# Decode attention over two caches: engine programs rolled into loops over the 16 groups, with TensorE's first matmuls at the end of its program

## The chip, the cores and the metric

The kernel runs on one core of a Trainium2 chip. The metric is the device time of one execution in microseconds; every time below is in microseconds unless it says ns. A core has five engines that run their own instruction streams and meet on semaphores: TensorE (PE, matmuls into PSUM), VectorE (DVE), ScalarE (ACT), GpSimd (POOL) and SyncE (SP), which here issues nearly all transfers. Sixteen DMA engines, fed by a queue in the order of issue, carry the data.

## The reference

Two halves, A and B, do the same on data of their own: one token attends over 8192 cached positions with 32 heads of 128, and the two results of 512 numbers are put side by side.

```python
def _A_ref(x, k_cache, v_cache, wq, wo):      # B the same, with its own five inputs
    q = (x @ wq).reshape(B, Sq, H, Dh).transpose(0, 2, 1, 3)      # 1 x 32 heads x 1 x 128
    scores = jnp.einsum("bhqd,bhkd->bhqk", q, k_cache) * (Dh ** -0.5)
    p = _softmax(scores, axis=-1)
    o = jnp.einsum("bhqk,bhkd->bhqd", p, v_cache)
    return o.transpose(0, 2, 1, 3).reshape(B, Sq, H * Dh) @ wo    # 4096 -> 512
```

All inputs are bf16. The caches are 67 MB each, four of them; the weights `wq` and `wo` are 4 MB each, four of them.

## The kernel before

**Tiles.** Four heads make a group, so there are 16 groups (`NM`), eight for A and eight for B. A group's K (or V) is one tile of 128 partitions, 32 for each head, with 256 positions of 128 numbers on each partition: one transfer of 8 MB. Two K tiles are in the buffer `kn`, one V tile in `vn`. Below, K3 is the K tile of group 3, wqA the projection weights of A.

**One group n.** VectorE multiplies the K tile by the broadcast query in place, in four chunks of 64 positions (`plan_mul`, L353). TensorE adds up each chunk's products over the head dimension, 16 matmuls with the identity that leave 8 partial sums for a position (`plan_red`, L362). VectorE adds these eight (`plan_sr`, L373). Then come the maximum over a head (`plan_max`, `plan_gmax`: VectorE, a TensorE transpose, VectorE) and its broadcast (`plan_exp`: a small matmul, ScalarE), the four exponentials on ScalarE (L410), their sum (`plan_sum`, L415), the product with V on TensorE (`plan_pv`, L433, 64 matmuls), a ScalarE copy out of PSUM (`plan_acc`, L451), four turning matmuls (`plan_turn`, L459) and the scaling on VectorE (`plan_o`, L465).

**The start.** wqA and x come first; x is spread over the partitions with matmuls; the queries of A are made with `plan_q` (L331), in two halves of 16 matmuls. Each matmul fills only the 32 columns of one head slice, so that the four slices stand side by side in the array. ScalarE copies a half to `qbc` in one cast (L339). The queries of B are made in the middle of group 0, after its third reduction.

**The end.** A's output and the first 16 heads of B are multiplied by `wo` while the last V is on its way, with the accumulating rows packed four to the array (`plan_wo`, L533); the remaining heads follow as rows of a second layout (`plan_wo_rows`, L572), and VectorE writes the last row for the store.

**What sets the order.** A plan (`_Plan`) records the operations with what they need, and `_Loop` folds the recorded rounds into loops. On SyncE the order is wqA, x, K0, wqB, K1, V0, K2, V1, K3, V2 and so on. K(n+1) waits for the last reduction of group n-1, which frees its buffer; V(n) waits for the product with V(n-1), which frees `vn`. TensorE's order in a round is: three reductions of group n, the sum and value product of group n-1, the fourth reduction of group n, the turning matmuls of n-1, the maximum. Around the loops of VectorE and ScalarE stands a loop of two passes, of which the first skips its body; TensorE has a similar one of two passes.

```python
            plan_red(n, 2)
            plan_sr(n, 1)
            plan_mul(n, 3)
            plan_sr(n, 2)
            if n == 0:
                for j in range(QA // 4):
                    plan_q(1, j)
            else:
                plan_sum(n - 1)
                for t0, t1 in zip(VLAST, VLAST[1:]):
                    plan_pv(n - 1, t0, t1)
                plan_acc(n - 1)
            plan_red(n, 3)
```

Of the kernel before, what the change touches and what calls it, by code (L numbers as in the profile page):

```python
# [11 lines left out]
P = 128  # L12


class _Ctr:


    def __init__(self, nc, stack, name):
        self.sem = stack.enter_context(nc.semaphore(name))
        self.n = 0  # L20
        self.name = name


class _Plan:


    def __init__(self):
        self.prog = {"SP": [], "PE": [], "ACT": [], "DVE": [], "POOL": []}
        self.waited = {}

    def wait(self, eng, mark):
        if mark is None:
            return
        ctr, val = mark
        if val <= 0 or self.waited.get((eng, ctr.name), 0) >= val:
            return
        self.waited[(eng, ctr.name)] = val
        self.prog[eng].append((None, ctr, val))

    def op(self, eng, fn, ctr=None, needs=(), inc=1):  # L40

        for m in needs:
            self.wait(eng, m)
        self.prog[eng].append((fn, ctr, inc))
        if ctr is None:
            return None
        ctr.n += inc
        return ctr, ctr.n


def _emit(e, items, slot=None):
    for fn, ctr, k in items:
        if fn is None:
            e.wait_ge(ctr.sem, k)
        elif isinstance(fn, tuple):
            which, fns = fn
            if slot is None:
                fns[which](e).then_inc(ctr.sem, k)
            else:
                with e.If_eq(slot, 0):  # L60
                    fns[0](e).then_inc(ctr.sem, k)
                with e.Else():
                    fns[1](e).then_inc(ctr.sem, k)
        elif ctr is None:
            fn(e)
        else:
            fn(e).then_inc(ctr.sem, k)


def _steps(items):  # L70


    out, waits = [], []
    for it in items:
        if it[0] is None:
            waits.append(it[1:])
        else:
            out.append((waits, it))
            waits = []
    assert not waits  # L80
    return out


class _Loop:


    def __init__(self, e, rounds):
        self.e = e
        rounds = [_steps(r) for r in rounds]
        assert len({len(r) for r in rounds}) == 1  # L90
        early, self.body, self.last = [], [], []
        for k in range(len(rounds[0])):
            at = [r[k] for r in rounds]
            assert all(it[1:] == at[0][1][1:] for _, it in at)
            first, second, third = at[0][0], at[1][0], at[2][0]
            waits = []
            for (ctr, v), (_, w) in zip(second, third):
                d = w - v
                assert v - d >= 1
                waits.append((ctr, v - d, d))  # L100
            for n, (ws, _) in enumerate(at[1:], 1):
                assert [(c, v) for c, v in ws] == [(c, v + n * d) for c, v, d in waits]
            for ctr, v in first:
                same = [x for c, x, _ in waits if c is ctr]
                if not same:
                    early.append((None, ctr, v))
                else:
                    assert v <= same[0]
            self.body.append((waits, at[0][1]))
            self.last.append([(c, v + len(rounds) * d) for c, v, d in waits])  # L110
# [19 lines left out]
def bass_concat_heads__mha_block_cached__gqa_block_cached__decode_kernel(  # L130
# [47 lines left out]
    with ExitStack() as st:  # L178
# [64 lines left out]
        def ctr(name):  # L243
            return _Ctr(nc, st, name)
# [518 lines left out]
```

## Time and profile before

| what | value |
|---|---|
| median of 3 runs | 666.33 (666.32 to 666.51) |
| the profiled execution's own time | 666.81 |
| its span, first to last instruction | 665.6 |
| VectorE busy | 341.2 (51% of the span) |
| TensorE matmuls busy, weight loads busy | 377.9 (57%), 176.0 (26%) |
| ScalarE busy | 71.8 (11%) |
| bytes read from HBM | 285.21 MB, 429 GB/s over the span |
| mean granted TensorE clock | 0.796 of full speed |

A row of the page names a line of the kernel, an engine, an operation, what it writes and reads, and how many there were; behind the bar stand the busy time, the mean of one in ns, and the idle time just before it with what ended it. `vn<-in_B_v_cache_dram` is a transfer of B's V cache into `vn`; SPq is SyncE's own queue of issues. A shape such as `128*16 128x512` for a matmul is the stationary operand, then the moving one.

### The profile page before, as it was taken

The page shows a single profiled execution, that of the slowest core. Times are in us where ns is not written, and L with a number is a line of the kernel's source. Part 1 is how long each engine was busy: PE and PEld are TensorE (multiplying, and loading weights), DVE is VectorE, ACT ScalarE, POOL GpSimd, SP SyncE. Part 2 cuts the span into 40 slices and gives each one's busy share as a digit, 9 for nine tenths or more (in the row PEclk, how much of TensorE's full clock was granted, in tenths as well). Part 3 has the DMA queues.
Part 4 walks back from the last instruction along what each step waited for, and adds up shares of the span by engine and source line. Part 5 has one row for each costly group of instructions (what it writes and reads, how often), then busy time and mean ns, then how long its engine had stood idle before and what let it go on. Part 6 is the DMA issues. An engine that isn't in the chain of part 4 may idle for free.

```text
span 665.6 us, 6342 instructions
## 1 busy us (share of the span) xinstructions
PE 377.9 (57%) x2569; PEld 176.0 (26%) x2569; DVE 341.2 (51%) x220; ACT 71.8 (11%) x167; POOL 3.0 (0%) x15
## 2 busy tenths in 40 slices
PE   1165755828285582828557281845738184573854
PEld 0022332403132241313224131322413132231422
DVE  1095817456281845638184563818456380835630
ACT  1002020010202011020201002020100202020020
POOL 1000000000000000000000000000000000000000
PEclk9998886959687695968779596877959687795987
DMA  9999999999999999999999999999999999999997
GB/s 380 435 447 434 434 438 437 410 429 441 437 437 437 437 437 418 421 441 441 433 437 437 441 425 410 441 441 433 437 437 441 433 410 433 441 437 433 412 437 302
DMA packets 6069, 285.31 MB, mean 429 GB/s; under 512 B 683, under 2 KB 942, under 8 KB 1198
## 3 DMA queue, kind: packets, MB, share of 16 engines
q1 hardware_dynamic: 6056, 285.22, 99.3%
q8 instruction: 4, 0.07, 0.0%
q14 instruction: 3, 0.02, 0.0%
q10 hardware_dynamic: 6, 0.00, 0.0%
HBM read 285.21 MB, written 0.00 MB: 429 GB/s over the span
## 4 chain that ended last, share of the span: by engine, by line
DMA 40%; PE 29%; DVE 15%; another core or an unknown queue 13%; issue 2%; SPq 0%; DVEq 0%; ACT 0%
PE rps L362 20%; DMA vn<-in_A_v_cache_dram 16%; DVE kn L353 13%; DMA vn<-in_B_v_cache_dram 10%; PE acc L433 8%; DMA kn<-in_A_k_cache_dram 7%; DMA kn<-in_B_wo_dram 5%; DMA kn<-in_B_x_dram 2%; DVE s_sb L373 1%; DVE m L379 1%; PE mtp L385 1%; SPq L256 0%; PE misc L415 0%; ACT xb L317 0%
## 5 line engine op out<-in xcount | busy, mean ns | idle before, releaser
L362 PE MATMUL rps<-kn,ident 128*128 128x512 bf16 x1024 | 265.6, 422 | 242.4 <-DVE kn L353 242.4
L353 DVE TENSOR_TENSOR kn<-kn,qbc 128x8192 bf16<-128x8192 bf16 x64 | 281.5, 4419 | 169.1 <-DMA kn<-in_A_k_cache_dram 89.2
L362 PEld LDWEIGHTS rps<-kn,ident 128*128 128x128 bf16 x1024 | 105.2, 107 | 396.2 <-issue 305.4
L373 DVE TENSOR_REDUCE s_sb<-rps 128x64 f32<-128x512 f32 x64 | 44.0, 688 | 118.0 <-PE rps L362 118.0
L433 PE MATMUL acc<-vn,pt 128*16 128x512 bf16 x1024 | 59.7, 386 | 10.9 <-DMA vn<-in_B_v_cache_dram 10.2
L451 ACT COPY xb<-acc 128x512 f32<-128x512 f32 x16 | 9.4, 585 | 438.6 <-PE acc L433 438.6
L410 ACT ACTIVATE pt<-s_sb,negb 32x256 bf16<-32x256 f32 x64 | 54.8, 857 | 1.9
L433 PEld LDWEIGHTS acc<-vn,pt 128*16 128x16 bf16 x1024 | 24.3, 91 | 39.0 <-DMA vn<-in_B_v_cache_dram 9.6
L398 PE MATMUL bmp<-gm,hrow 1*128 1x1 f32 x128 | 17.8, 256 | 6.0 <-DVE gm L388 6.0
L398 PEld LDWEIGHTS bmp<-gm,hrow 1*128 1x128 f32 x128 | 16.5, 197 | 10.7 <-DVE gm L388 10.0
L459 PEld LDWEIGHTS bmp<-tsel,xb 128*128 128x128 f32 x128 | 16.7, 191 | 3.3 <-ACT xb L451 1.2
L410 ACT ACTIVATION_READ_ACCUMULATOR pt<-s_sb,negb 32x1 f32 x64 | 15.9, 248 | 0.0
L459 PE MATMUL bmp<-tsel,xb 128*128 128x4 f32 x128 | 15.3, 243 | 0.7 <-ACT xb L451 0.7
L402 ACT ACTIVATE negb<-bmp 128x1 f32<-128x1 f32 x16 | 2.7, 171 | 97.1 <-PE bmp L398 97.1
L465 DVE TENSOR_TENSOR oD<-bmp,rinv 128x4 f32 (+1 forms) x16 | 2.4, 153 | 16.6 <-PE bmp L459 16.6
L385 PE MATMUL mtp<-ident_f,m 128*1 128x128 f32 x32 | 6.1, 270 | 8.0 <-DVE m L379 8.0
L313 PE MATMUL misc<-ones_bf,kn 1*128 1x128 bf16 x4 | 0.6, 304 | 13.0 <-DMA kn<-in_B_x_dram 13.0
L388 DVE TENSOR_REDUCE gm<-mtp 1x4 f32<-1x128 f32 x16 | 4.5, 279 | 6.5 <-PE mtp L385 6.5
L331 PE MATMUL qyp<-vn,xb 128*32 128x512 bf16 x64 | 6.0, 504 | 2.2 <-ACT qbc L339 1.5
L379 DVE TENSOR_REDUCE m<-s_sb 128x1 f32<-128x256 f32 x16 | 6.7, 420 | 0.5
L415 PEld LDWEIGHTS misc<-rsum,ones_f 128*128 128x128 f32 x32 | 6.0, 190 | 2.9 <-issue 0.7
L339 ACT CAST qbc<-qyp 128x512 bf16<-128x512 f32 x4 | 2.3, 586 | 38.7 <-PE qyp L331 38.7
(58 smaller groups left out, 39.3 us busy)
## 6 DMA issues: line engine op xcount, KB each, us to landing
vn<-in_B_v_cache_dram SPq DMA_DIRECT2D x1, 6144.0 KB, 24.6
vn<-in_A_wq_dram SPq DMA_DIRECT2D x1, 4096.0 KB, 13.1
vn<-in_B_wq_dram SPq DMA_DIRECT2D x1, 4096.0 KB, 40.6
kn<-in_A_wo_dram SPq DMA_DIRECT2D x1, 4096.0 KB, 41.1
kn<-in_B_wo_dram SPq DMA_DIRECT2D x1, 2048.0 KB, 45.7
vn<-in_B_v_cache_dram SPq DMA_DIRECT2D x1, 2048.0 KB, 29.1
kn<-in_B_wo_dram SPq DMA_DIRECT2D x1, 1024.0 KB, 31.1
kn<-in_B_wo_dram SPq DMA_DIRECT2D x1, 512.0 KB, 31.9
```

What stands on the lines that cost most here:

```text
L331: r = e.matmul(qyp[hh * HP:(hh + 1) * HP, :].rearrange("p (i d) -> p i d", d=Dh), xb[:, a, c, hh * HP:(hh + 1) * HP], w, start=(c == 0), s ...
L353: mul_done[n, c] = op("DVE", lambda e: e.tensor_tensor(k, k, qbc[:, nth(n), :].broadcast_to([P, CT, Dh]), ALU.mult), c_mul, [k_in[n], qbc_ ...
L362: r = e.matmul(rps[:, c % 2, :].rearrange("p (t d) -> p t d", d=DW), ident[:], kn[:, i0, c * CT:(c + 1) * CT, i * DW:(i + 1) * DW], start= ...
L373: sr_done[n, c] = op("DVE", lambda e: e.tensor_reduce(s_sb[:, c * CT:(c + 1) * CT], rps[:, c % 2, :].rearrange("p (t d) -> p t d", d=DW), ...
L379: m_done[n] = op("DVE", lambda e: e.tensor_reduce(m1[:], s_sb[:], AX.X, ALU.max), c_dve, [sr_done[n, NCH - 1]])
L385: m = op("PE", lambda e: e.matmul(mtp[0:1, 0:P], m1[:], ident_f[:], start=True, stop=True), c_pe, [m_done[n], i_identf, gm_done.get(n - 1)])
L398: r = e.matmul(bmp[:, 0:1], hrow[0:1, (G - 1 - h) * HP:(G - 1 - h) * HP + P], gm[0:1, h:h + 1], start=(h == 0), stop=(h == G - 1))
L410: p_done[n] = op("ACT", lambda e, h=h, q=q: e.activation(pt[q, :, h], s_sb[q, :], AF.Exp, bias=negb[q, n:n + 1], scale=scale, accum_out=rs ...
L415: m = op("PE", lambda e: e.matmul(misc[:, 0:G], ones_f[:], rsum[:], start=True, stop=True), c_pe, [p_done[n], misc_free[0]])
L433: r = e.matmul(acc[q:q + NT * G, :], pt[:, ts, :].rearrange("p t g -> p (t g)"), vn[:, ts, :].rearrange("p t d -> p (t d)"), start=(j < NP ...
L451: acc_read[n] = op("ACT", lambda e: e.copy(acc_sb, acc[:]), c_act, [pv_done[n], turned.get(n - 1)])
L459: r = e.matmul(bmp[:, NT:NT + G], acc_sb[:, t * Dh:(t + 1) * Dh], tsel[:, t * G:(t + 1) * G], start=(t == 0), stop=(t == NT - 1))
```

## The change

The plan and its loop folder go; each engine's program is written out by hand as a loop over the groups. What moves:

- **TensorE's program** begins with a jump to the block `pe_first`, which stands at the end of the program. There x is spread and the queries of A and of B are made, both, in loops. Then it jumps back to `pe_main`. A query matmul now fills all 128 columns, with a PSUM bank for each of the four head slices, and ScalarE takes them to `qbc` in four casts of 32 partitions.
- **In the main loop** all four reductions of group n stand ahead of the sum and value product of group n-1. A chunk is one matmul and then five passes of three, with addresses from a register.
- **The maximum** is one VectorE operation with a transposing write (`gm`, L436), with no TensorE trip; it stands behind the scaling of group n-1.
- **SyncE:** wqB waits until wqA has landed; K(n+1) waits for the first multiplication of group n in place of the last reduction of group n-1; K1 thus waits for K0's first multiplication, and x has a place of its own behind the two K tiles. V(n) waits for the same as before.
- **The end:** the rows of `wo` are accumulated in one PSUM row, one matmul of one column after another in a loop of four, and are not packed; ScalarE copies the two rows.
- The two-pass loops around the engines' programs are gone, and several constants with them.

In the rows below a row is an instruction in program order with what it writes and reads, its shape and the semaphores it waits on.

TensorE before, from the start of its program: `misc` and `qyp` hold the spread x and the queries, `rps` the partial sums.

```order
L313 MATMUL qyp<-ones_bf,kn 128x128 x4
L331 MATMUL qyp<-vn,xb 32x512 [waits s_w0,c_act]
...
L362 MATMUL rps<-kn,ident 128x512 [waits c_mul,c_pool]
...
L362 MATMUL rps<-kn,ident 128x512 [waits c_mul]
...
L362 MATMUL rps<-kn,ident 128x512 [waits c_sr,c_mul]
...
L331 MATMUL qyp<-vn,xb 32x512 [waits c_act,s_w1]
```

TensorE of the change, at the end of its program, which it runs first: `big` holds the queries, `acc_sb` the spread x.

```order
L326 MATMUL tps<-ones_bf,kn 128x128 x4
L330 UNCONDITIONAL_BRANCH [waits s_xb]
L332 REGISTER_ALU [waits s_w]
...
L336 MATMUL big<-vn,acc_sb 128x512
...
L342 ISA [waits s_qc]
L333 COMPARE_AND_BRANCH
...
L330 COMPARE_AND_BRANCH
L343 UNCONDITIONAL_BRANCH
```

The three reductions that stood between the two halves' queries now follow both, behind the last jump.

TensorE before, inside its loop over the groups, from the third reduction on (each reduction is there twice, once for each K buffer): `misc` takes the sum, `acc` the value product.

```order
L60 COMPARE_AND_BRANCH [waits c_sr,c_mul]
L362 MATMUL rps<-kn,ident 128x512 x16
...
L415 MATMUL misc<-rsum,ones_f 128x4 [waits c_act]
L127 REGISTER_ALU
L433 MATMUL acc<-vn,pt 16x512 [waits s_v0]
...
L722 COMPARE_AND_BRANCH
L60 COMPARE_AND_BRANCH [waits c_sr,c_mul]
L362 MATMUL rps<-kn,ident 128x512 x16
```

TensorE of the change at the same place: a chunk's first matmul, the pass of three, and what follows the four chunks.

```order
L242 ISA [waits s_sr,s_mul]
L244 ISA
L244 MATMUL big<-kn,ident 128x512
L245 UNCONDITIONAL_BRANCH
L231 ISA
L247 MATMUL big<-kn,ident 128x512
...
L250 ISA
L245 COMPARE_AND_BRANCH
L251 ISA
L239 COMPARE_AND_BRANCH
...
L286 MATMUL misc<-rsum,ones_f 128x4 [waits s_p]
L294 MATMUL acc<-vn,pt 16x512 [waits s_v]
```

The sum and the value product moved from between the third and fourth reductions to behind the fourth, and a chunk became a loop with register instructions and a jump.

SyncE before, from wqB on:

```order
L256 DMA vn<-in_B_wq_dram 128x16384
L256 DMA kn<-in_A_k_cache_dram 128x32768 [waits c_act]
L256 DMA vn<-in_A_v_cache_dram 128x32768 [waits c_pe]
L256 DMA kn<-in_A_k_cache_dram 128x32768 [waits c_red]
L256 DMA vn<-in_A_v_cache_dram 128x32768 [waits c_pv]
```

SyncE of the change at the same place:

```order
L170 DMA vn<-in_B_wq_dram 128x16384 [waits s_w]
L170 DMA kn<-in_A_k_cache_dram 128x32768 [waits s_mul]
L170 DMA vn<-in_A_v_cache_dram 128x32768 [waits s_q]
L170 DMA kn<-in_A_k_cache_dram 128x32768 [waits s_k,s_red]
L170 DMA vn<-in_A_v_cache_dram 128x32768 [waits s_pv]
```

The order of the transfers is kept; what they wait for is not. The core of the diff, with the removed classes and planning functions left out:

```diff
-        kn = sb("kn", [P, NK, T, Dh], BF16)
+        kn = sb("kn", [P, 2 * T + 1, Dh], BF16)
...
+        load_k(0)
+        load_wq(1, (s_w, 16))
+        for n in range(NM):
+            if n + 1 < NM:
+                load_k(n + 1, *([(s_red, RED), (s_k, 32)] if n == 1 else [(s_mul, NCH * n + 1)]))
+                load_v(n, (s_pv, n + 1) if n else (s_q, 4 * NA * 2))
+        load_wo(0, 0, H, s_woA, (s_mul, NCH * (NM - 1) + 1))
+        load_wo(1, *WOB[0], s_wo[0])
...
+        nc.br("pe_first", engines=[nc.tensor.engine])
+        with nc.body("pe_main", valid_engines=[nc.tensor.engine]):
...
+            with e.Fori(0, NM + 1) as n:
...
+                    with e.Fori(0, NCH) as c:
+                        e.wait_ge(s_mul, k1)
+                        e.wait_ge(s_sr, k1)
...
+                        e.matmul(o, ident[:], chunk(0), start=True, stop=False, skip_group_check=True)
+                        with e.Fori(0, RL):
+                            for u in range(RU):
+                                i = e.matmul(o, ident[:], chunk((1 + u) * DW), start=False,
+                                             stop=(u == RU - 1), skip_group_check=True)
+                            i.then_inc(s_red, 1)
+                            e.reg_add(ko, ko, RU * DW)
...
+                with e.If_ne(nr, 0):
+                    e.wait_ge(s_p, n1)
+                    e.matmul(misc[:, 0:G], ones_f[:], rsum[:], start=True, stop=True).then_inc(s_sum, 1)
+                    e.wait_ge(s_v, rv)
...
+        with nc.body("pe_first", valid_engines=[nc.tensor.engine]):
...
+            e.wait_ge(s_xb, NA)
+            with e.Fori(0, NA) as a:
+                e.wait_ge(s_w, rw)
+                e.reg_add(rw, rw, 16)
+                with e.Fori(0, 2) as j:
+                    with e.Fori(0, G) as hh:
+                        for c in range(C):
+                            i = e.matmul(
+                                big[:, bass.ds(hh, 1), :].rearrange("p o (i d) -> p (o i) d", d=Dh),
+                                xb[:, a, c, :], wq_v[:, a, c, j, :, hh, :],
+                                start=(c == 0), stop=(c == C - 1))
+                        i.then_inc(s_q, 1)
+                    e.wait_ge(s_qc, rq)
+                    e.reg_add(rq, rq, G)
+            nc.br("pe_main", engines=[nc.tensor.engine])
...
+            mul(0)
+            mul(1)
+            e.wait_ge(s_p, n1)
+            sr(0)
+            mul(2)
+            sr(1)
+            mul(3)
+            sr(2)
+            sr(3)
+            e.wait_ge(s_sr, ks)
+            e.tensor_reduce(m1[:], s_sb[:], AX.X, ALU.max).then_inc(s_m, 1)
+            e.wait_ge(s_sum, n1)
+            e.reciprocal(rinv[:], misc[:, 0:G]).then_inc(s_ri, 1)
+            e.wait_ge(s_ri, n1)
+            e.wait_ge(s_turn, n1)
+            e.tensor_tensor(oD_all[:, bass.ds(n * G, G)], tps[:, 0:G], rinv[:],
+                            ALU.mult).then_inc(s_o, 1)
+            e.wait_ge(s_m, n1)
+            e.tensor_reduce(gm[:], m1[:].broadcast_to([P, 32]), AX.X, ALU.max, negate=True,
+                            apply_transpose=True).then_inc(s_gm, 1)
```

`s_mul`, `s_red` and `s_sr` count the multiplications, the passes of the reductions and the partial sums; `s_pv` counts the value products, with one put there at the start. `mul` and `sr` are the former `plan_mul` and `plan_sr`, with the buffer and the query row taken from registers.

More of the change, by code (lines that the diff above doesn't have):

```diff
@@ L12 @@
 P = 128
[L15 to L48, printed above, removed]
@@ L51, in _emit @@
[L51 to L67, printed above, removed]
@@ L296, in load_wq @@
[L296 to L303 removed]
+        g = nc.gpsimd
+        g.memset(ones_bf[:], 1.0).then_inc(c_on, 1)
```

796 lines of the change are left out of this document (292 added, 504 removed).

## The prediction

> **What bounds the kernel now.** I read the page's slices and queues first. In these rows a digit is the busy tenth of a slice of 16.6 us, and GB/s is what the sixteen DMA engines moved.
>
> ```profile
> span 665.6 us, 6342 instructions
> ...
> DMA  9999999999999999999999999999999999999997
> GB/s 380 435 447 434 434 438 437 410 429 441 437 437 437 437 437 418 421 441 441 433 437 437 441 425 410 441 441 433 437 437 441 433 410 433 441 437 433 412 437 302
> ...
> q1 hardware_dynamic: 6056, 285.22, 99.3%
> ```
>
> The reader is to see one queue that is never dry. No engine's own work sets the end; the end is head + 285 MB + tail, and any stretch in which SyncE has issued nothing ahead adds its whole length. So I asked next when each early transfer is issued and when it lands: SyncE's timeline, then the DMA issues, each with the microseconds to its landing in the last column.
>
> ```profile
> 2.28 0.51 SPq L256 DMA_DIRECT2D vn<-in_B_wq_dram  x1
> 14.78 0.33 SPq L256 DMA_DIRECT2D kn<-in_A_k_cache_dram  x1
> 55.20 0.33 SPq L256 DMA_DIRECT2D vn<-in_A_v_cache_dram  x1
> 58.70 0.33 SPq L256 DMA_DIRECT2D kn<-in_A_k_cache_dram  x1
> 86.80 0.33 SPq L256 DMA_DIRECT2D vn<-in_A_v_cache_dram  x1
> ```
> ```profile
> vn<-in_A_wq_dram SPq DMA_DIRECT2D x1, 4096.0 KB, 13.1
> vn<-in_B_wq_dram SPq DMA_DIRECT2D x1, 4096.0 KB, 40.6
> kn<-in_A_k_cache_dram SPq DMA_DIRECT2D x1, 48.5
> vn<-in_A_v_cache_dram SPq DMA_DIRECT2D x1, 27.4
> kn<-in_A_k_cache_dram SPq DMA_DIRECT2D x1, 43.3
> vn<-in_A_v_cache_dram SPq DMA_DIRECT2D x1, 34.5
> ```
>
> Issue plus landing gives the clock of the queue: wqB 42.9 (the projection weights of half B), K1 63.3 (K of group 1), V0 82.6, K2 102.0, V1 121.3. One group's K or V takes 19.3. V1 is issued at 86.8, 15 us before the queue would be empty. The edit is safe wherever an issue keeps such a lead.
>
> **The steady loop.** Here is one group where the engines wait for the data (the last K, landed at 605.12).
>
> ```profile
> 605.12 8.76 DVE L353 TENSOR_TENSOR kn<-kn,qbc 128x8192 bf16<-128x8192 bf16 x2 [10.21 <-DMA kn<-in_B_k_cache_dram]
> ...
> 616.33 0.69 DVE L373 TENSOR_REDUCE s_sb<-rps 128x64 f32<-128x512 f32 x1 [2.44 <-PE rps L362]
> 616.93 4.42 DVE L353 TENSOR_TENSOR kn<-kn,qbc 128x8192 bf16<-128x8192 bf16 x1
> ...
> 621.87 4.42 DVE L353 TENSOR_TENSOR kn<-kn,qbc 128x8192 bf16<-128x8192 bf16 x1
> 624.90 0.41 PEld L415 LDWEIGHTS misc<-rsum,ones_f 128*128 128x128 f32 x2
> ...
> 625.32 3.63 PE L433 MATMUL acc<-vn,pt 128*16 128x512 bf16 x64
> ...
> 629.00 0.80 SPq L256 DMA_DIRECT2D vn<-in_B_v_cache_dram  x2
> ...
> 632.55 0.69 DVE L373 TENSOR_REDUCE s_sb<-rps 128x64 f32<-128x512 f32 x1 [5.58 <-PE rps L362]
> ...
> 634.17 0.28 DVE L388 TENSOR_REDUCE gm<-mtp 1x4 f32<-1x128 f32 x1 [0.40 <-PE mtp L385]
> ```
>
> The four products end at 626.29 = landing + 21.2. Now the value product stands behind the fourth reduction: 21.2 + 0.15 hand-over + 3.63 reduction + 0.42 sum + 3.68 = landing + 29.05, against 23.9. So V(n) goes out 5.2 us later; the K in front of it ends at landing + 38.6, and the lead stays 9.5. K(n+1), which now waits for the first product, goes out at landing + 4.5, and the V in front of it ends at + 19.3. Both later issues cost nothing: the queue covers them. For the last V the cover is shorter:
>
> ```profile
> 593.38 0.43 SPq L256 DMA_DIRECT2D kn<-in_B_wo_dram  x1
> ```
> ```profile
> kn<-in_B_wo_dram SPq DMA_DIRECT2D x1, 2048.0 KB, 45.7
> ```
>
> The wo transfer ahead of it ends at 593.38 + 45.7 = 639.1; the last V would go out at 634.2. A lead of 4.9, still nothing. The shorter route to the maximum (no TensorE round trip) lies in DVE's idle time and brings nothing either.
>
> **The start.** Here the lead is lost. Before, three reductions of group 0 ran while wqB was in flight, and B's projections were four head slices side by side:
>
> ```profile
> 33.23 8.76 DVE L353 TENSOR_TENSOR kn<-kn,qbc 128x8192 bf16<-128x8192 bf16 x2 [26.74 <-DMA kn<-in_A_k_cache_dram]
> ...
> 37.81 9.19 PE L362 MATMUL rps<-kn,ident 128*128 128x512 bf16 x32 [18.41 <-DVE kn L353]
> ...
> 48.66 3.63 PE L362 MATMUL rps<-kn,ident 128*128 128x512 bf16 x16 [1.67 <-DVE kn L353]
> ...
> 52.22 1.08 PE L331 MATMUL qyp<-vn,xb 128*32 128x512 bf16 x16
> ...
> 68.14 9.39 PE L362 MATMUL rps<-kn,ident 128*128 128x512 bf16 x32 [6.37 <-DVE kn L353]
> ```
>
> Now no reduction starts before both projections are done. Prices, with three rows of the chain of waits (start, length, piece) and one of another group: a set of 16 full-width matmuls takes 5.95 where TensorE had been idle for 6.37, and 3.63 (0.227 for one) where it had not; two casts take 1.08, so four about 2.05; a hand-over from a product to its reduction is 0.16, or 0.30 where a jump is taken on the way, so 0.15 for the jump.
>
> ```profile
> 13.68 1.08 ACT xb L317 x2
> 67.84 0.30 issue
> 68.14 5.95 PE rps L362 x16
> ...
> 183.97 0.16 issue
> ```
>
> - Projections of B: 42.9 + 5.95 + 2.05 + 3.63 = 54.5, plus 0.5 for hand-overs: V0 goes out at 55.0 as before (55.20). Then 2.05 of casts and 0.3 for the jump: the first reduction starts at R = 57.4 instead of 37.81. A's projections take the same 14 us from 14.8, done by 29, ahead of K0 at 33.2; K1 goes out at 37.7, 5.2 ahead of wqB's end. Both free.
> - Group 0: R + 3.63, 0.6, 4.94, 4.42 (fourth product ends at R + 13.6), 0.15, 3.63: K2 goes out at R + 17.4 = 74.8, ahead of V0's end at 82.6. From the start of the last partial sum to the end of `gm` it was 632.55 to 634.45, 1.9; with one more small operation and without the trip to TensorE I take 2.0: VectorE is free at R + 19.4 = 76.8. K1 had landed at 63.3.
> - Group 1: 76.8 + 29.05 = 105.9, plus 0.6 for four loop entries at 0.15: **V1 goes out at 106.5, K2 landed at 102.0.** The queue is dry, and K3 stands behind V1 on SyncE.
>
> What a transfer costs that starts on an empty queue has no row in the middle of the run. The nearest are wqA at the start, whose 13.1 are 3.45 more than half of 19.3 (it has half the bytes), and SyncE's wait for the small store at the end (total, times, longest):
>
> ```profile
> SPq L734 <- DMA out_dram<-out_q: 1.0, 1, 1.0
> ```
>
>  I take 2.2, and keep 1.0 and 3.45. V1 then lands at 106.5 + 19.3 + 2.2 = 128.0 instead of 121.3: **6.7 us**. After it K3 (out at 111) and V2 (out about 138, K3 ends at 147) have leads again, and DMA at its ceiling gives nothing back.
>
> **The end.** The last wo lands, then 16 matmuls, a copy and the store: kept. The row that must be ready first has little room:
>
> ```profile
> 662.40 0.16 DVE L494 COPY oz<-oD 128x2 bf16<-128x2 bf16 x1
> ...
> 663.07 0.81 PE L572 MATMUL yrow<-kn,oz 128*32 128x128 bf16 x16 [0.39 <-DMA kn<-in_B_wo_dram]
> ```
>
> Ready at 662.56, used at 663.07. A loop exit (0.15 to 0.3) and two more waits on DVE eat that: 0 to 1, taken 0.2. The 48 output matmuls of one column each are not packed by four any more: 48 × 0.227 = 10.9. They follow the loop's last value product (landing of the last K + 29.05) with some 3.5 of turning and spreading ahead and 3 of copies behind: done at + 46.5. The first three quarters of the last V land behind the wo at 639.1 + 0.75 × 19.3 = 653.6, + 48.5: free, and up to 3 if the clock is low.
>
> **Unknown: the matmul loops.** Each pass of three matmuls has four register instructions and a jump.
>
> ```profile
> 63.27 0.09 DVEq L353
> ```
>
> At 0.09 each, plus 0.15 and three matmuls at 3.63/64 = 0.057, a pass needs 0.68 us of TensorE's sequencer; the array needs 3 × 0.227 = 0.68. So about hidden, taken as nothing; at twice the price a reduction takes 5.1, 1.5 more, and four of them stand in the chain to V1: 0 to 6 us.
>
> **Sum.** 6.7 + 0.2 = 6.9 on the profiled 666.81: 673.7. The median of the runs is 666.33, so I forecast **673.2**.
>
> **The clock.** After 1.67 us of idleness TensorE ran on at full pace (3.63 for 16, row 48.66), after 6.37 it started at a lower one (5.95). R comes after about 2.4 of idleness, between them and nearer to the first; I take full pace, and the slower start would add 2.3. [...]
>
> **Rivals.**
> - *The clock never falls* (not slower). If TensorE's denser work kept it up from wqB on, 2.3 go from the first projection and 2.44 (DVE's idle time in row 616.33) from group 1: V1 goes out at 101.8, and with 1.0 for the empty queue it lands at 122.1: 0.8 late, 667.3 with the tail. It decides from an issue at 101 to 102 on. Against it: the 5.95 after 6.37 of idleness. Chance 0.09.
> - *The loops are sequencer-bound, or a jump stalls*: 6 more on the chain; the last V, with two such reductions ahead, goes out at 637.2, and its 1.0 to 3.45 use up the lead to 639.1 or 1.6 more; a stalled jump adds up to 1.3. Time 679 to 682. The price of a stall is bounded by the queue that loads code, 4 packets at 0.0%, so under 0.05% × 16 × 665.6 / 4 = 1.3 us each.
>
> ```profile
> q8 instruction: 4, 0.07, 0.0%
> ```
>
> [...] No row of this profile shows such a stall. Chance of this rival 0.12.
> - *The change does not do what it says, or the gap is absent and the tail is shorter*: 663.07 to 665.6 is 2.5, of which 1 at most could go: 665.3. Chance 0.03.
>
> **How the numbers follow.** Forecast 0.76, rivals 0.09, 0.12, 0.03. A measurement of this kernel tells 0.2% (1.3 us) from no change. Forecast and second rival are slower: 0.88; the first is the same: 0.09; the third faster: 0.03. The forecast's own bounds: 1.0 for the empty queue gives 672.0, and a clock that rises half as late in the two slow sets (1.2 less in each) 669.6; 3.45 and the slower start at R give 676.8. The range takes in most of the loops' bound and stops short of the first rival: 668.5 to 682.
>
> **What would show it.** DMA below 9 in slice 6 (100 to 116 us) and nowhere else; V1's issue at 104 to 111, first reduction near 57, group 1's first product near 77, K2's landing still 102; steady leads of 9 and more; the start of the last matmuls to the end within 0.5 of 2.5. I am wrong in mechanism if V1 goes out before 100 or the lost time lies elsewhere.

## The result, and the profile after

| | before | after |
|---|---|---|
| median | 666.38 (666.32 to 666.51, 4 runs) | 683.96 (683.11 to 685.43, 4 runs) |
| the profiled execution's own time | 666.81 | 683.11 |
| its span | 665.6 | 681.9 |

After to before is 1.0266, with a 95% interval of 1.0247 to 1.0285: slower by 17.6. The prediction was 673.2 with a range up to 682.0. Direction, place and mechanism are as predicted; the size is some 2.5 times what I gave, and the time lies beyond the range. The profiled execution is the fastest of the four. It is 16.3 longer than that of before, and this is what I account for below.

Two corrections to the description of the change. x did not get a place of its own: it still lies at the start of the second K buffer, and K1's wait for K0's first multiplication is what keeps it until it has been read. And K2 is an exception to the rule for K(n+1): it waits for the last reduction of group 0 (and for K1's landing), as in the kernel before.

First the page of the changed kernel, its 40 slices (17 us each) and its queues.

```profile
span 681.9 us, 8031 instructions
...
DMA  9999793999999999999999999999999999999997
GB/s 382 429 467 427 327 423 115 434 442 431 431 431 431 431 431 431 431 431 431 431 431 431 431 438 450 438 442 434 442 431 431 431 431 431 431 431 431 423 442 304
...
q1 hardware_dynamic: 6056, 285.22, 97.1%
q8 instruction: 1, 0.02, 0.0%
```

Before, no slice but the last was below 9. Now the fifth has a 7 and the seventh a 3; from the eighth on the queue is full again. The transfers fall behind in one stretch, near the start. SyncE's timeline names the transfers there (K1 at 38.13, V0, K2, V1, K3):

```profile
38.13 0.33 SPq L170 DMA_DIRECT2D kn<-in_A_k_cache_dram  x1
58.20 0.33 SPq L170 DMA_DIRECT2D vn<-in_A_v_cache_dram  x1
83.20 0.33 SPq L170 DMA_DIRECT2D kn<-in_A_k_cache_dram  x1
114.94 0.33 SPq L170 DMA_DIRECT2D vn<-in_A_v_cache_dram  x1
122.09 0.33 SPq L170 DMA_DIRECT2D kn<-in_A_k_cache_dram  x1
```

The DMA issues give 21.9 from V1's issue to its landing, and 21.9 for K2:

```profile
vn<-in_A_v_cache_dram SPq DMA_DIRECT2D x1, 21.9
```

K2 lands at 83.20 + 21.9 = 105.1, V1 at 136.8; before, V1 landed at 121.3. The busy time in windows of 2 us (the last two columns are the share of the DMA engines and GB/s, with each packet counted where it begins) shows what lies between:

```profile
104.00:106.00 2.00, 1.64 (x7) 0.57 (x6) 2.00 (x2) 0.00 (x0) 0.00 (x0) 1.00 0.00 0
106.00:108.00 2.00, 1.61 (x7) 0.67 (x7) 0.62 (x2) 0.00 (x0) 0.00 (x0) 1.00 0.00 0
...
112.00:114.00 2.00, 2.00 (x44) 0.92 (x40) 0.00 (x0) 0.00 (x0) 0.00 (x0) 1.00 0.00 0
114.00:116.00 2.00, 1.31 (x24) 0.62 (x12) 0.00 (x0) 0.59 (x1) 0.00 (x0) 1.00 0.59 197
```

In the DMA records K2's last packet ends at 104.8 and V1's first begins at 115.9: 11.1 us without transfers, while TensorE is busy for most of the time. The chain to V1's issue is at work and is too long. A shorter stretch of 2.8 us lies at 81.4, ahead of K2.

Nothing is added afterwards in the steady part. The last K's products begin at

```profile
620.87 8.76 DVE L408 TENSOR_TENSOR kn<-kn,qbc  x2 [6.18 <-DMA kn<-in_B_k_cache_dram]
```

against 605.12: 15.75 later, V1 was 15.5 later. The store goes out at 680.54 against 664.25, 16.3 later. So the loss has two places: 15.5 at V1 and about 0.8 behind it, most of it at the end.

### The profile page after: what moved, and what is told of

It is laid out like the page before. It is cut to its first block, busy times and chain, and to the rows that moved or that the text cites. A ratio compares the mean times of both kernels' runs of the same rounds, so it can differ in the third digit from the quotient of the medians.

```text
span 681.9 us, 8031 instructions
## 1 busy us (share of the span) xinstructions
PE 405.0 (59%) x2407; PEld 169.9 (25%) x2407; DVE 338.9 (50%) x218; ACT 80.9 (12%) x182; POOL 2.4 (0%) x13
## 4 chain that ended last, share of the span: by engine, by line
DMA 74%; DVE 13%; PE 9%; issue 2%; ACT 1%; DVEq 0%; ACTq 0%; SPq 0%
DMA kn<-in_B_k_cache_dram 40%; DMA kn<-in_A_k_cache_dram 25%; DVE kn L408 12%; PE big L247 5%; DMA vn<-in_B_wq_dram 4%; DMA vn<-in_B_v_cache_dram 3%; DMA vn<-in_A_wq_dram 2%; PE big L336 2%; PE acc L294 1%; PE big L244 1%; ACT qbc L359 1%; PE tps L300 0%; PE yrow L219 0%; DVE s_sb L413 0%; DVEq L403 0%
## 5 line engine op out<-in xcount | busy, mean ns | idle before, releaser
L408 DVE TENSOR_TENSOR kn<-kn,qbc x64 | 281.5, 4419 | 123.5 <-DMA kn<-in_A_k_cache_dram 65.6
L247 PE MATMUL big<-kn,ident 128*128 x960 | 272.4, 431 | 0.0
L244 PE MATMUL big<-kn,ident 128*128 x64 | 28.5, 445 | 216.7 <-DVE kn L408 212.2
L247 PEld LDWEIGHTS big<-kn,ident 128*128 128x128 bf16 x960 | 103.6, 108 | 153.6 <-issue 101.0
L413 DVE TENSOR_REDUCE s_sb<-big 128x64 f32<-128x512 f32 x64 | 44.1, 689 | 115.4 <-PE big L247 115.4
L365 ACT COPY acc_sb<-acc 128x512 f32<-128x512 f32 x16 | 9.4, 586 | 478.8 <-PE acc L294 478.8
L244 PEld LDWEIGHTS big<-kn,ident 128*128 128x128 bf16 x64 | 6.3, 99 | 234.0 <-issue 231.8
L336 PE MATMUL big<-vn,acc_sb 128*128 x64 | 21.1, 497 | 22.8 <-DMA vn<-in_B_wq_dram 13.4
L300 PE MATMUL tps<-tsel,acc_sb 128*128 128x4 f32 x128 | 17.7, 262 | 11.0 <-ACT acc_sb L365 10.4
L300 PEld LDWEIGHTS tps<-tsel,acc_sb 128*128 128x128 f32 x128 | 16.3, 199 | 19.3 <-ACT acc_sb L365 17.9
L359 ACT CAST qbc<-big 32x512 f32 x16 | 9.2, 577 | 36.6 <-PE big L336 36.3
L269 PE MATMUL big<-kn,o 128*1 x48 | 12.4, 421 | 0.0
```

What stands on the lines that cost most here:

```text
L244: e.matmul(o, ident[:], chunk(0), start=True, stop=False, skip_group_check=True)
L247: i = e.matmul(o, ident[:], chunk((1 + u) * DW), start=False, stop=(u == RU - 1), skip_group_check=True)
L269: i = e.matmul(y, o2[:, bass.ds(h + u, 1)], wo_sb[:, h + u, :], start=False, stop=False, skip_group_check=True)
L300: i = e.matmul(tps[:, 0:G], acc_sb[:, t * Dh:(t + 1) * Dh], tsel[:, t * G:(t + 1) * G], start=(t == 0), stop=(t == NT - 1))
L336: i = e.matmul(big[:, bass.ds(hh, 1), :].rearrange("p o (i d) -> p (o i) d", d=Dh), xb[:, a, c, :], wq_v[:, a, c, j, :, hh, :], start=(c = ...
L359: e.copy(qbc[q, bass.ds(j * 4, 4), :].rearrange("p i d -> p (i d)"), big[q, hh, :]).then_inc(s_qc, 1)
```

## The experiments

**The theory under test.** The start of the chain is a sum: projections, hand-overs, group 0, group 1, value product. V1 lands 22.0 after its issue once the queue is empty by then, and at 121 if it is issued early enough; in between, an issue at 99.5 (experiment 7) landed 23.2 later. Every microsecond by which V1 lands late is one of the time, and the end adds up to about 0.8. I take the parts as independent, so that each can be taken out alone and its price read at V1's issue. Against it stand, by experiment: that the register loops slow every reduction; that the low clock alone is the cause; that the moved work costs time by itself, wherever the queue stands.

Unless said otherwise an edit is made to the changed kernel, and the profiles are single executions. Where no number of runs is given, the time is that of the profiled execution alone. On the chips of these runs the kernel before took 666.66 (the first four, and the last two) and 666.34 (median of 25 runs, for the four others).

**1 (a_pv). The value product back between the third and fourth reductions.**

```diff
-                    with e.Fori(0, NCH) as c:
...
+                    with e.Fori(0, NCH - 1) as c:
+                        red(big[:, bass.ds(c % 2, 1), :].rearrange("p o (t d) -> p (o t) d", d=DW))
...
                     i.then_inc(s_pv, 1)
+                with e.If_lt(nr, NM):
+                    red(big[:, 1, :].rearrange("p (t d) -> p t d", d=DW))
```

> The changed kernel with the sum and value product of group n-1 put back between the third and the fourth reduction of group n; all else as changed. Theory 1 (the whole loss is the one late issue of V1, which the queue has to wait for): V1 goes out some 4.6 earlier, at about 110, the second stretch without transfers shrinks by as much, and the time falls to about 679. Theory 2 (the loss is spread over the groups, by the slower loops): one thing that happens in each of 16 groups is undone, so the time between K tiles in the steady part would fall; with 19.35 for a tile before and after, theory 2 has little left. Theory 3 (the first gap, where K2 is late, costs by itself): K2 still goes out at 83, so 2.8 stay lost however V1 moves.

Measured: 680.59. TensorE's rows, the value product and the reduction that now follows it:

```profile
108.98 3.63 PE L295 MATMUL acc<-vn,pt 128*16 128x512 bf16 x64
112.55 0.39 PE L239 MATMUL big<-kn,ident 128*128 x1
```

V1 went out at 112.66, later than the 110 expected, because B's two sets of projections took 6.03 and 6.36 in this execution and the first reduction came at 64.61, 1.9 later than in the changed kernel's profile. From group 1's first product to V1's issue it took 25.1 (87.52 to 112.66) instead of 29.6 (85.38 to 114.94). The move costs 4.4 on the chain, near the 5.2 of the prediction.

**2 (a_static). The projections written out instead of looped.** Width and casts stay.

```diff
-            with e.Fori(0, NA) as a:
-                e.wait_ge(s_w, rw)
...
+            for a in range(NA):
+                e.wait_ge(s_w, 16 * (a + 1))
+                for j in range(2):
+                    for hh in range(G):
```

> The changed kernel with the four projection rounds written out instead of looped, so that no register instruction or jump stands between the casts and the next matmuls; full width and four casts as changed. If the hand-overs of 1.0 and 2.1 and the clock that they lose are part of the chain to V1: first reduction near 58.5 instead of 62.7, V1 at 108 to 110, time 677 to 679. If they are not on the chain: 683 to 685 as before.

Measured: 680.10; V1 out at 112.07, landed at 133.87. TensorE's rows (the second set of B's projections, then the first reduction):

```profile
51.90 3.63 PE L332 MATMUL big<-vn,acc_sb 128*128 128x512 bf16 x16 [2.57 <-ACT qbc L353]
59.73 0.60 PE L243 MATMUL big<-kn,ident 128*128 x1 [4.20 <-issue]
```

The second set runs at full pace, 3.63, and follows the casts almost at once (2.57 idle, of which the casts are 2.38). In this pair the loops cost 3.0 at the first reduction (62.74 against 59.73), though wqB landed 0.8 later here (43.9 against 43.2). The stretch without DMA ahead of K2 is gone, and that brings nothing by itself: V1 still lands 21.8 after its issue, 12.6 late.

**3 (a_warm). Ten matmuls of no use behind each round of projections,** to keep the clock up; they write a bank that is not in use.

```diff
+            e.wait_ge(c_pool, POOL)
...
                         i.then_inc(s_q, 1)
+                    for _ in range(10):
+                        e.matmul(yrow, ones_bf[:], flat(pt[:])[:, 0:512], start=True, stop=True,
+                                 skip_group_check=True)
```

> The changed kernel with ten more matmuls without use (zeros, into a bank that is written later) behind each projection round, while TensorE waits for the casts. They only keep TensorE busy. If the lower clock of the second round and of the first reductions is what made them 5.6 and 6.0: those fall to about 3.9, V1 goes out at 109 to 111, time 678 to 680. If the pace is that of the loops' register instructions: no gain, 683 to 686.

Measured: 682.72; V1 out at 113.47. One pass of the second set, and the first reduction:

```profile
56.18 1.02 PE L337 MATMUL big<-vn,acc_sb 128*128 x4 [0.30 <-issue]
...
63.10 0.39 PE L244 MATMUL big<-kn,ident 128*128 x1 [2.41 <-issue]
63.38 3.94 PE L247 MATMUL big<-kn,ident 128*128 x15
```

With TensorE kept busy (the matmuls of no use take 2.11 from 50.03 and again from 58.59) the first reduction takes 4.2 instead of 5.9, but the start of that reduction does not move (63.10 against 62.74): a looped pass of four takes 1.33 here as in the change (52.53 to 53.86, below), the first set took 0.7 longer in this execution (5.68 against 4.98), and the rest is hand-overs. The edit gives back 1.5 at V1's issue, less than the 4 to 6 expected. That is not the whole price of the clock: group 1's first reduction, after 7.00 of idleness, still took 5.6 (5.8 in the change, at a granted clock of 0.50 from 87.8 to 94.6).

**4 (a_ru15). One pass of fifteen matmuls instead of five of three** in a reduction.

```diff
-    RU = 3
+    RU = 15
```

> The changed kernel with one pass of fifteen matmuls in a reduction in place of five passes of three (4 jumps fewer per reduction). If a pass is bound by TensorE's sequencer (0.78 measured against 0.68 of matmuls), a reduction on a running TensorE falls from 4.2 to 3.7, and with one or two such on the chain to V1 the time falls by 0.5 to 1.5; if the register instruction ahead of each matmul binds, nothing moves.

Measured: 685.27; V1 out at 117.03. A reduction that finds TensorE running and does not queue behind another falls from 4.15 (at 132.96 in the change) to 3.63 (at 135.67 here), what one written out takes (3.63 at 48.66 before): the four passes more, with their register instructions and jumps, cost 0.5. It gains nothing where it counts: two slow sets of projections (6.41 and 6.56) put this execution's first reduction at 65.54, and from there to V1 it took 51.5 against 52.2. The loops of the reductions are some 0.7 of the chain in this pair.

**5 (b_both). The kernel before, with only the order of the change:** B's projections ahead of group 0's reductions, the value product behind the fourth.

```diff
             plan_mul(n, 0)
+            if n == 0:
+                for j in range(QA // 4):
+                    plan_q(1, j)
             plan_red(n, 0)
...
-            if n == 0:
-                for j in range(QA // 4):
-                    plan_q(1, j)
-            else:
+            if n > 0:
+                plan_red(n, 3)
...
                 plan_sum(n - 1)
...
-            plan_red(n, 3)
+            if n == 0:
+                plan_red(n, 3)
```

> The kernel before, with the two moves of order alone: B's projections ahead of group 0's reductions, and the value product behind the fourth reduction; projections still four heads side by side, reductions still written out. Theory 1 (only an issue of V1 later than the queue's end costs): the first reduction near 48, group 1 starts near 67, V1 goes out near 96, before K2 lands at 102: no stretch without transfers, 666.0 to 667.0. A rival that blames the order as such (a reduction set or value product late in each group) expects a loss already here.

Measured: 666.55 (666.16 to 667.47, 10 runs), ratio 1.0003 (0.9994 to 1.0013): no difference. SyncE's rows for V0, K2 and V1:

```profile
47.67 0.33 SPq L256 DMA_DIRECT2D vn<-in_A_v_cache_dram  x1
66.36 0.33 SPq L256 DMA_DIRECT2D kn<-in_A_k_cache_dram  x1
96.72 0.33 SPq L256 DMA_DIRECT2D vn<-in_A_v_cache_dram  x1
```

V1 goes out 9.9 later than before (96.72 against 86.80) and lands at 121.1 all the same. The lead pays for the order moves, whole.

**6 (a_narrow). Narrow projections:** written out, 32 columns for each head slice, side by side in one bank, and one cast.

```diff
-                                big[:, bass.ds(hh, 1), :].rearrange("p o (i d) -> p (o i) d", d=Dh),
-                                xb[:, a, c, :], wq_v[:, a, c, j, :, hh, :],
...
+                            i = e.matmul(big[q, 0, :].rearrange("p (i d) -> p i d", d=Dh),
+                                         xb[:, a, c, q], wq_v[:, a, c, j, :, hh, :],
...
-            for hh in range(G):
-                q = slice(hh * HP, (hh + 1) * HP)
-                e.copy(qbc[q, bass.ds(j * 4, 4), :].rearrange("p i d -> p (i d)"),
-                       big[q, hh, :]).then_inc(s_qc, 1)
...
+            e.copy(qbc[:, bass.ds(j * 4, 4), :].rearrange("p i d -> p (i d)"),
+                   big[:, 0, :]).then_inc(s_qc, 1)
```

> The changed kernel with the projections written out and four heads side by side again (32 columns each, one cast per round), everything else as changed. Theory 1: V0 goes out near 50, the first reduction at 51 to 53, V1 at 103 to 106, so about 5 of lateness stay and the time is 671 to 675. If the full width is not on the chain: 680, as with the rounds only written out.

Measured: 671.25; V1 out at 102.91, landed at 124.91. TensorE's rows:

```profile
43.63 1.93 PE L333 MATMUL big<-vn,acc_sb 128*32 128x512 bf16 x16 [24.17 <-DMA vn<-in_B_wq_dram]
46.37 1.93 PE L333 MATMUL big<-vn,acc_sb 128*32 128x512 bf16 x16 [0.81 <-ACT qbc L352]
50.72 0.61 PE L243 MATMUL big<-kn,ident 128*128 x1 [2.41 <-issue]
```

A set is 1.93 and a cast under 0.8. The first reduction comes 9.0 earlier than with full-width sets written out (59.73), V1 9.2 earlier. Of the 9.0, the rows give 5.0 to the sets (5.23 and 3.63 against twice 1.93), 3.5 to the casts, and 0.5 to a first set that began earlier in this execution. Only the two moves of order together (9.9) cost more.

**7 (a_narrow_pv). Edits 6 and 1 together.**

```diff
+            e.copy(qbc[:, bass.ds(j * 4, 4), :].rearrange("p i d -> p (i d)"),
+                   big[:, 0, :]).then_inc(s_qc, 1)
...
+                with e.If_lt(nr, NM):
+                    red(big[:, 1, :].rearrange("p (t d) -> p t d", d=DW))
```

> The same with the value product back between the third and fourth reductions as well. Theory 1, with lateness that adds up until the queue's end: V1 at 98 to 101, a gap of 0 to 2, time 666.5 to 669. If each undone part keeps a price of its own in the steady part: the sum of single gains (about 10 and 4.5) and no floor, below 667.

Measured: 666.67 (666.07 to 668.51, 10 runs), ratio 1.0004 (0.9994 to 1.0014). In the profiled execution, the slowest of the ten (668.51), V1 went out at 99.51 and landed at 122.7. The time of before is back, though the jump, the loops of the reductions, the unpacked `wo` rows and the new maximum are all still there.

**8 (a_fix). Edit 7, and wqB loaded ahead of K0** without the wait for wqA, with semaphores of their own. K1 then waits only until x has been read, in place of K0's first multiplication.

```diff
-        load_k(0)
-        load_wq(1, (s_w, 16))
+        load_wq(1, s_w1)
+        load(flat(kn[:, 0:T, :]), quad(ks, 0), s_k0)
```

> The same again, with B's projection weights loaded ahead of K0 (a semaphore of its own for each of the first transfers), so that both projections are done before K0 lands. Theory 1: first reduction at 48, V1 near 95, no gap; time 666.3 to 667.8, where what is left over 666.4 is the end (its TensorE steps at the lower clock, 0.8).

Measured: 666.44 (665.92 to 666.84, 10 runs), ratio 1.0002 (0.9992 to 1.0011); V1 out at 95.69, landed at 120.9. A larger lead buys nothing more: the queue is full from start to end, and there is no version here that beats the kernel before.

**9 (a_wq). Edit 2, with wqB ahead of K0 and K1's wait as in 8;** full-width sets and the late value product stay.

```diff
-                e.wait_ge(s_w, rw)
...
+                e.wait_ge((s_w, s_w1)[a], 16)
...
-        load_k(0)
-        load_wq(1, (s_w, 16))
+        load_wq(1, s_w1)
+        load(flat(kn[:, 0:T, :]), quad(ks, 0), s_k0)
```

> The changed kernel with its projections written out (full width and four casts kept) and B's projection weights loaded ahead of K0; value product behind the fourth reduction as changed. Theory 1: the projections are done near 46, the first reduction waits for K0's first multiplication and starts near 48.5; V1 goes out 52.2 later as in the runs so far, near 100.7, and lands 22.0 behind that: 1 to 2 late, time 667 to 669. If full width cost by itself wherever it stands: 671 or more.

Measured: 669.00. TensorE's first reduction and SyncE's issue of V1:

```profile
48.97 0.60 PE L245 MATMUL big<-kn,ident 128*128 x1 [8.44 <-DVE kn L406]
```
```profile
100.64 0.33 SPq L171 DMA_DIRECT2D vn<-in_A_v_cache_dram  x1
```

The same long projections, begun earlier, end in the shadow of K0's transfer: TensorE waits for VectorE, not the other way round. V1 lands at 122.5, 1.2 late, and the end adds 0.9 (store 543.9 after V1's landing, 543.0 before): 2.1 for a measured 2.3.

**10 (a_tail). Ten matmuls of no use ahead of the wait for the last quarter of the last V,** to keep the clock up at the end.

```diff
                             with e.If_eq(nr, NM):
+                                for _ in range(10):
+                                    e.matmul(zps, ones_bf[:], zb[:, 0:1, :].broadcast_to([P, 4, P]),
+                                             start=True, stop=True, skip_group_check=True)
                                 e.wait_ge(s_v1, 16)
```

> The changed kernel with ten matmuls without use ahead of its wait for the last quarter of the last V. They only keep TensorE busy there. If the rest of the loss (16.3 in the span, 15.5 in V1's landing, so 0.8) is the lower clock of the last steps: the turning matmuls fall from 1.9 to 1.05 and the two rows of 32 from 1.04 to 0.6, and from the landing of that quarter to the store's issue it takes 5.4 to 5.7 in place of 6.6. If it is the longer program there: no change.

Measured: 685.19, which says little by itself, since V1 went out at 117.35 in this execution. What it tells is the end. TensorE's last matmuls in before, in the change, and in this kernel:

```profile
658.74 1.04 PE L433 MATMUL acc<-vn,pt 128*16 128x512 bf16 x16 [0.93 <-DMA vn<-in_B_v_cache_dram]
660.47 1.06 PE L459 MATMUL bmp<-tsel,xb 128*128 128x4 f32 x8 [0.69 <-ACT xb L451]
661.45 0.63 PE L572 MATMUL yrow<-kn,oz 128*32 128x128 bf16 x32
```
```profile
674.24 1.32 PE L294 MATMUL acc<-vn,pt 128*16 128x512 bf16 x16 [2.35 <-DMA vn<-in_B_v_cache_dram]
676.24 1.87 PE L300 MATMUL tps<-tsel,acc_sb 128*128 128x4 f32 x8 [0.68 <-ACT acc_sb L382]
...
679.13 1.04 PE L219 MATMUL yrow<-kn,oz 128*32 128x128 bf16 x32
```
```profile
674.64 2.33 PE L292 MATMUL big<-zb,ones_bf 128*128 128x512 bf16 x10
677.04 1.04 PE L297 MATMUL acc<-vn,pt 128*16 128x512 bf16 x16
678.77 1.05 PE L303 MATMUL tps<-tsel,acc_sb 128*128 128x4 f32 x8 [0.69 <-ACT acc_sb L385]
...
681.39 0.85 PE L219 MATMUL yrow<-kn,oz 128*32 128x128 bf16 x16 [0.30 <-DMA kn<-in_B_wo_dram]
```

The change waits 2.35 for the last V where before waited 0.93, and then runs at a lower clock (granted 0.50 from 678.1 to 680.2, where before had 1.00 from 657 to 663; 1.87 for the turning matmuls against 1.06). With the matmuls of no use ahead the turning takes 1.05, and the last matmuls wait for `wo` again, as before. From the landing of the last part of `wo` to the store's issue it took 0.72 before (663.53 to 664.25), 1.44 in the change (679.10 to 680.54) and 0.71 here (681.91 to 682.62): a TensorE kept busy is worth 0.7 of the 0.8 at the end. From the landing of V's last quarter to the store it took 5.8, a little over the 5.4 to 5.7 expected, and 6.6 in the change.

**All of them in one table.** "First reduction" is the start of group 0's; "sum" is 666.8 + (V1 landed − 121.3) + 0.8, or 666.8 where V1 lands by 121.3.

| kernel | first reduction | V1 out | V1 landed | sum | measured |
|---|---|---|---|---|---|
| before | 37.81 | 86.80 | 121.3 | | 666.8 |
| 8: narrow, product back, wqB first | 48.76 | 95.69 | 120.9 | 666.8 | 666.3 |
| 5: order only | 47.51 | 96.72 | 121.1 | 666.8 | 667.4 |
| 7: narrow, product back | 50.88 | 99.51 | 122.7 | 669.0 | 668.5 |
| 9: full width, wqB first | 48.97 | 100.64 | 122.5 | 668.8 | 669.0 |
| 6: narrow | 50.72 | 102.91 | 124.9 | 671.2 | 671.3 |
| 2: written out | 59.73 | 112.07 | 133.9 | 680.2 | 680.1 |
| 1: product back | 64.61 | 112.66 | 134.5 | 680.8 | 680.6 |
| 3: useless matmuls | 63.10 | 113.47 | 135.3 | 681.6 | 682.7 |
| the change | 62.74 | 114.94 | 136.8 | 683.1 | 683.1 |
| 4: RU = 15 | 65.54 | 117.03 | 139.2 | 685.5 | 685.3 |
| 10: clock kept at the end | 64.83 | 117.35 | 139.3 | 684.8 | 685.2 |

(Measured is the profiled execution's own time; for 10 the sum has no end. The 0.8 was taken from the change, whose row therefore agrees by construction.) Over 30 us of V1's issue the sum holds within 0.6, but for kernel 3, which was 1.1 longer; 2.0 lie between its last landing and the store, 0.6 more than in the change, and the rest stays open. The steps between neighbours price the change at V1's issue, on one execution each: order 9.9 (before to 5), the rest of the rewrite, with the rolled reductions and the jump in it, 6.2 (5 to 6), full-width sets and four casts 9.2 (6 to 2), loops around the sets 2.9 (2 to the change). These prices are rough: the change and kernels 1, 4 and 10 run the same program up to the first reduction and started it at 62.74, 64.61, 65.54 and 64.83, so the 2.9 could as well be 5. Together they are 28.1. The lead before was 15.2 (102.0 − 86.8), and a transfer that starts on an empty queue lands 2.6 later than one in the stream (21.9 against 19.35): 28.1 − 15.2 + 2.6 = 15.5.

## Why the prediction was right and wrong

**Right: what bounds, and where it breaks.** One queue, dry between K2 and V1 and full again from K3 on; steady part unchanged; value product later and harmless in the steady loop; K1's later wait free. I named V1's issue as the term that decides, and it does. Not foreseen was the short stretch at 81.4, which put K2 at 105.1 instead of 102.0 and costs nothing by itself (experiment 2).

**Wrong: the sum to V1's issue.** I gave 106.5; it was 114.94, and the other times of the chain that I had named came late as well: the first reduction (near 57) at 62.74, group 1's first product (near 77) at 85.38, K2's landing (102) at 105.1. The working breaks at two of its three steps. TensorE's and ScalarE's rows of the change for the first:

```profile
44.00 4.98 PE L336 MATMUL big<-vn,acc_sb 128*128 x16 [13.36 <-DMA vn<-in_B_wq_dram]
52.53 1.02 PE L336 MATMUL big<-vn,acc_sb 128*128 x4 [3.54 <-issue]
53.86 4.31 PE L336 MATMUL big<-vn,acc_sb 128*128 x12 [0.30 <-issue]
62.74 0.60 PE L244 MATMUL big<-kn,ident 128*128 x1 [4.57 <-issue]
63.14 5.46 PE L247 MATMUL big<-kn,ident 128*128 x15
```
```profile
49.12 2.38 ACT L359 CAST qbc<-big 32x512 f32 x4 [15.97 <-PE big L336]
58.30 2.38 ACT L359 CAST qbc<-big 32x512 f32 x4 [6.80 <-PE big L336]
```

- *"Plus 0.5 for hand-overs", "0.3 for the jump".* The first reduction was to start at 57.4 and started at 62.74, 5.3 later. Of this 3.4 are hand-overs: 0.8 were budgeted, 4.2 were there (0.84 from wqB's landing at 43.16 to the first matmul, 1.03 from the casts to the next round, 2.06 from the last cast at 60.68 to the reduction, 0.27 at the two starts of the casts). I had priced one jump by a row of a running engine; this path leaves three nested loops, jumps, and enters two more. The sets add 1.0 (4.98 and 5.64 for 5.95 and 3.63: the second runs in a loop, which I did not work out for the projections at all, and at a granted clock of 0.50 from 53.63 to 57.05; it took 5.0 in kernel 3, where TensorE was kept busy, and 3.63 in kernel 2, written out), the casts 0.7 (2.38 for 2.05), and wqB's landing 0.3.
- *Group 0, "R + 19.4".* 22.6, 3.2 more. "I take full pace, and the slower start would add 2.3": the first reduction took 5.9 instead of 3.63, at a granted clock of 0.50 (the clock's rows below). I held the bound in the text and chose the wrong end of it. The longer hand-overs made 4.57 of idleness out of my 2.4, but it is not shown that 2.4 would have kept the clock: it fell at 60.46, 2.3 after the last projection, and in kernel 6 the same reduction took 5.8 after 2.41. The third reduction was slow too (4.91 for 15, at a granted clock of 0.50 from 74.11 to 77.53), and a product hands over in 0.36, not 0.15.
- *Group 1, 29.05 + 0.6.* 29.56: right, partly by luck: the products ended 0.55 sooner than in my row, and the fourth reduction took 0.56 longer (4.19 for 3.63).
- *"2.2" for an empty queue.* 21.9 from issue to landing against 19.35 for a tile in the stream, 2.6: right within its bounds.
- *The end, "taken 0.2".* 0.8, by the clock (experiment 10). I had bounded it by 0 to 1.

So 5.3 + 3.2 − 0.1 + 0.4 + 0.6 = 9.4 is the whole distance from my 673.7 to 683.1. The mechanism was right, and the term that was mis-sized is the chain from wqB's landing to group 0's last reduction: its hand-overs (4.2 for 0.8) and its first reduction (5.9 for 3.63) before all. The range failed for the same reason: the mis-sized terms all lie in one chain with no cover left, so they add. The rival that allowed 6 us more for loops gave 679 to 682, nearer than my own, and I gave it 0.12; it came near for another reason than its own.

**On the loops.** The rival charged the loops of the *reductions*; those are some 0.7 of the chain (experiment 4). The loops that cost are those around the projections, with the entries between rounds (2.9 in the pair of experiment 2).

**On the clock.** I had the clock as a single choice of 2.3. The column ahead of the last two is the granted clock of the change, here around the first reduction at 62.74:

```profile
57.05:60.46 3.41, 1.12 (x5) 0.29 (x3) 0.00 (x0) 2.08 (x4) 0.00 (x0) 1.00 0.85 365
60.46:67.29 6.83, 4.55 (x11) 1.68 (x12) 0.00 (x0) 0.81 (x2) 0.00 (x0) 0.50 1.05 441
```

In the clock records of the change, as in those of before, the granted clock is 0.50 or 1.00, and its changes lie a multiple of 3.41 us apart (here 46.81, 53.63, 57.05, 60.46, 67.29). The same code took different times in different executions: the two sets of B's projections 4.98 and 5.64 in one profile and 6.41 and 6.56 in another (kernel 4, same code there), and the change's four runs spread over 2.3 where those of before lie within 0.2. What decides when the clock rises, no run shows. Before, such scatter fell into the lead; now it reaches the time. Nor does idleness alone, by which the prediction chose, settle when it falls: it fell behind a stretch of 3.41 us in which TensorE had been busy for 1.12 (first row), and behind others with 1.02 and 1.36 (50.22 to 53.63, 70.70 to 74.11), while it stayed at 1.00 behind one with 1.41 (98.01 to 101.42).

## What to carry to other kernels

When one queue sets the time, write down for each early transfer how much earlier than needed it is issued, and treat that lead as a budget that all edits share: none of the four steps here (9.9, 6.2, 9.2, 2.9) would have used up the lead of before by itself, and together they spent nearly twice as much. Once the lead is gone, small terms (loop entries, a clock that starts low, one more cast) stop hiding and add up one for one, and the range should be made from their sum, not from the largest. Rolling a program into loops cost next to nothing where the engine waits for data anyway (the last K's products came 15.75 later, V1 15.5); a short serial stretch ahead of the first transfers is better written out, or started earlier, as loading wqB ahead of K0 showed (kernel 9 against kernel 2: 669.0 for 680.1).

## What the runs showed of the hardware

- Entering the next round of a nested loop on TensorE took 1.03 from the last cast to the first matmul (the change, at 52.53), where the same round written out took 0.1 (kernel 2, at 51.90); the way out of the projection loops, back by the jump and into the main loop took 2.06 (to 62.74), and 1.7 without the loops (kernel 2, to 59.73).
- Around the jump back, at about 61 in the change, no packet stands on the queues that the page calls `instruction`: the one on `q8` came at 2.5, the one on `q14` at 681.7. A stall of the jump, which the second rival allowed for, no run here shows. What the 2.06 consist of stays open.
- A pass of three matmuls with addresses from a register takes 0.78 on a running TensorE (4.2 for the reduction from 106.39, granted clock 1.00), but a reduction that was queued behind another at a granted clock of 0.50 took 3.62, full pace (the second of group 0, from 68.43, granted 1.00 from 67.29 on). What makes the queued one faster, no run shows.
- Idleness alone does not tell the clock: after 2.41 idle the first reduction took 4.2 where TensorE had been kept busy (kernel 3) and 5.8 where two sets of 1.93 stood ahead (kernel 6). In kernel 6 the pace was low already ahead of the idleness: in the kernel before, the same 16 narrow matmuls took 1.08 at a granted clock of 1.00 (52.22).
- A transfer of 8 MB on an empty queue moved its first data 1.0 after the issue (V1 of the change, 114.94 to 115.9) and landed some 2.6 later than one in the stream (19.35), in each of the seven profiles in which V1 found the queue empty (21.8 to 22.1 from issue to landing).
